# A spectral filter mixed with a product-key memory layer: four of the early row tiles, not two, summed by accumulating TensorE transposes

## The chip, the cores and the metric

One core of a Trainium2 chip runs the whole program. Its engines are TensorE (PE), VectorE (DVE), ScalarE (ACT), GpSimd (POOL) and SyncE (SP); each works through its own queue in order, and they meet by semaphores. The metric is the device time in microseconds (us); the median of three runs is given for the kernel before.

## The reference, cut to what matters

The input x has 2048 rows of 576 numbers. Two branches are computed from it and mixed by a gate per row.

```python
g = sigmoid((x * gate_w).sum(-1))
a = irfft2(rfft2(x) * (w_r + 1j * w_i))               # branch A, over rows and columns
q = einsum("nd,dhc->nhc", x, w_q)                      # branch B: 32 heads, 2 x 128
s1, s2 = q[..., :128] @ k1.T, q[..., 128:] @ k2.T      # 64 scores each
i1, i2 = argmax(s1), argmax(s2);  e = i1 * 64 + i2     # one of 4096 experts per head
act = gelu(sum(x * u[e]));  w = softmax of one score (which is 1)
b = sum over heads of w * act * v[e]
out = g * a + (1 - g) * b
```

So each row and head needs one row of u (for a dot product with x) and one row of v (added, scaled, into the result).

## The kernel before

**Tiles.** The 2048 rows are 16 tiles of 128 rows, one per partition. The 32 heads are 8 chunks `c` of 4. Tiles 0 to 9 are *early* (`E_T`): their branch B runs while scores are still being computed. Tiles 10 to 15 are *late*: theirs runs afterwards, beside branch A.

**Scores.** `build_m` folds w_q and the keys into one matrix per chunk, kept as a high and a low part. `scores(c, tp)` computes chunk c for the two tiles of pair tp: ten *score parts* (`part`), eight of three and two of two 512-column matmuls, 640 parts in all. A reduce on DVE (L415) takes the maxima, ACT compares every score with its maximum (L422), and some DVE and ACT steps turn that into expert numbers (`ei`, `eil`).

**Early groups.** `group(t, c)` handles the four heads of a chunk for one early tile. POOL issues four gathers (L516, 128 rows of 4608 bytes, u and v side by side, into a buffer `uv`); DVE makes four dot products (L523); ACT takes the gelu (L525); a small step makes the four factors `a`. Then the v rows are summed, in one of three ways:

- *by DVE*: one scaled add per row (L553), or, where a bit of `ROWS[t][c]` is set, the row scaled in place by ACT (L548) and added by DVE (L549);
- *by a diagonal* (`is_d`: `ROWS[t][c]` is 16): ACT makes the factors (L535) and writes a 128 x 128 diagonal matrix per row (L563, buffer `dg`); TensorE multiplies it with the row, two matmuls of 288 columns, and accumulates in PSUM; DVE adds the group's sum to the tile's (L577);
- *by transposes* (`lean`, for the tiles in `T_T`): ACT scales the row in place (L499); TensorE transposes it in five pieces of 128 columns, accumulating over the four rows in PSUM; DVE adds the group's sum to a transposed accumulator `xw` (L506; the tile's first group is copied there by ACT, L504). At the end `mix` turns the accumulator back with five more transposes.

In PSUM there are four double banks, shared by all of this: a group by diagonals or by transposes keeps one from its first row to DVE's add.

**Late tiles.** `quad` gathers four rows for 32 tokens at a time (L604), makes the dot products (L609), a block matrix `dg` on DVE (L613), and sums on TensorE. All its gathers wait for the first part of the last score tile (`HELD`).

**Branch A.** `fold` (sums and differences of x, small matmuls), `unit` (transforms, the spectral weights `w`, transforms back) and `invert` (the last transform of a tile) run on TensorE with DVE and ACT between; `mix` and `send` finish a tile.

**Order.** A planner outside the program has fixed the order of all work: every call of `plan` is a job, numbered in program order, and `ORDER` lists the numbers. `follow` gives out buffers in that order, and each engine issues its own jobs in it, the DMAs of SP and POOL too. All matmuls go through the helper at L260, so they are told apart by their tiles: `mh, xt` scores, `dg` diagonals (128*128) and late sums (128*32), `ident,uv` transposes, `fi` transforms.

Of the kernel before, what the change touches and what calls it, by code (L numbers as in the profile page):

```python
# [15 lines left out]
P = 128  # L16
D = 576
# [137 lines left out]
def tile_kernel(ctx, tc, xn, xT, x5, wqT, wq5, kT, wri, uv, gw, t_kr, t_fi, t_tw, t_io, out):  # L155
# [26 lines left out]
    for tag, n in (('cand', 2), ('z', 8), ('b', 8), ('a', 8), ('im', 1), ('fe', 2), ('dg', 3)):  # L182
        ring(tag, 'sm', n)
    ring('uv', 'gp', NG)
    ring('xn', 'xp', 2 * NE - 2 * NPAIR - len(T_T))
    ring('p2', 'ps', 4)
# [299 lines left out]
    accs = {}  # L486
# [146 lines left out]
    def finish(t, pd, sum_of):  # L633

        y = accs[t] = buf(('xl', 'xn'), [P, D])
        ga = gas[t]
        for r in range(2):
            cols = slice(288 * r, 288 * r + 288)
            sum_of(r)
            dv(0.43, lambda r=r, cols=cols: stt(y.ap[:, cols], pd.ap[:, r, :288], gone[:, t:t + 1], ga.ap[:, cols], op0=ALU.mult, op1=ALU.add), [(y, r)], [(pd, r), (ga, 0), (ga, 1), 'gone'])  # L640
            ld(load(P * 1152, 1152), lambda cols=cols: nc.sync.dma_start(out[t][:, cols], y.ap[:, cols]), [], [(y, r)])
# [328 lines left out]
ROWS = {0: (0, 16, 16, 15, 6, 2, 12, 0), 1: (0, 15, 0, 12, 5, 16, 5, 16), 2: (12, 8, 2, 6, 0, 8, 0, 1), 3: (2, 10, 0, 5, 0, 7, 4, 16), 4: (4, 0, 0, 6, 16, 7, 16, 0), 5: (2, 0, 1, 0, 0, 9, 12, 16), 6: (4, 15, 4, 8, 16, 0, 16, 14), 7: (8, 0, 16, 16, 6, 12, 9, 2), 8: (6, 16, 7, 0, 12, 16, 16, 11), 9: (4, 0, 0, 16, 0, 8, 16, 5)}  # L970
SPLIT = 0
T_T = (0,1)
# [17 lines left out]
def is_d(t, c):  # L990
    return t < NE and ROWS[t][c] > 15


ORDER = [
# [214 lines left out]
```

## Time and profile before

| | |
|---|---|
| runs | 898.75, 900.19, 900.25 us; median 900.19 |
| profiled execution | 900.38 us; its span in the trace 898.6 us |
| busy in the span | PE 856.3, DVE 811.5, ACT 596.3, POOL 570.3 us |
| granted TensorE clock, mean | 0.984 |
| moved | 342.44 MB, of which 302.02 by the 512 gathers |

A row of a group of instructions has the line, engine, operation, output and inputs by name, shapes and count; then busy time in us, the mean ns of one, and the idle time of the engine before them. A row of the timeline has the start, the length, the engine, the line and the same names. Busy times overlap a little from one instruction to the next, so what an instruction costs its engine is read from the starts.

### The profile page before, as it was taken

Reading aid. Unit: us, or ns where it says so; the run is one execution under the profiler, and the core shown is the slowest. Engines: PE = TensorE matmul, PEld = TensorE weight load, DVE = VectorE, ACT = ScalarE, POOL = GpSimd, SP = SyncE. Lnnn points to the kernel's source line nnn. Section 1 sums busy time; section 2 is a strip of 40 time slices with the busy share of each in tenths; the row PEclk is TensorE's granted clock in tenths of the full one; section 3 lists DMA queues with packets and bytes.
Section 4 is the critical chain, followed back from the end, with each engine's and each line's share of the span. In section 5 each row is a group of like instructions: output and inputs, shape, how many; then the busy total and the mean of one; then the engine's idle time right before and its main releaser. Section 6 shows DMA issues by size and latency. Waiting matters only on the chain. (4 is left out here: it accounts for less than half of the span.)

```text
span 898.6 us, 16947 instructions
## 1 busy us (share of the span) xinstructions
PE 856.3 (95%) x5502; PEld 661.0 (74%) x5502; DVE 811.5 (90%) x2022; ACT 596.3 (66%) x2067; POOL 570.3 (63%) x516
## 2 busy tenths in 40 slices
PE   6999999999999999999999999769889999899987
PEld 5888888888888778888888888657556676566554
DVE  3779999999999899999999999899999889877877
ACT  4999997877878688788879789773232434232322
POOL 0356556666677676676657776666767677777771
PEclk9999999999999999999999999859999999999999
DMA  9999999999999999999999999999999999999998
GB/s 299 349 332 367 379 345 367 349 372 361 380 357 368 377 386 384 376 388 357 394 359 368 415 350 397 418 370 365 402 415 420 419 402 419 420 420 419 418 419 340
DMA packets 89611, 342.44 MB, mean 381 GB/s; under 512 B 9969, under 2 KB 10865, under 8 KB 89522
## 3 DMA queue, kind: packets, MB, share of 16 engines
q0 software_dynamic: 73728, 302.02, 86.5%
q1 hardware_dynamic: 15794, 39.33, 11.9%
q8 instruction: 44, 0.72, 0.3%
q14 instruction: 45, 0.37, 0.1%
HBM read 336.59 MB, written 4.72 MB: 380 GB/s over the span
## 5 line engine op out<-in xcount | busy, mean ns | idle before, releaser
L516 POOL DMA_INDIRECT uv<-uv,ei x317 | 356.6, 1125 | 226.5 <-issue 46.6
L260 PE MATMUL bank<-mh,xt 128*128 128x512 f32 x768 | 269.8, 402 | 0.0
L422 ACT ACTIVATE area<-bank,area 128x64 bf16<-128x64 f32 x1008 | 220.3, 360 | 15.1 <-DVE area L415 10.9
L604 POOL DMA_INDIRECT uv<-uv,eiq x144 | 156.6, 1087 | 70.1 <-issue 23.3
L523 DVE SCALAR_TENSOR_TENSOR uv<-uv,pair 128x576 f32<-128x576 f32 x256 | 187.3, 750 | 12.5 <-DMA uv<-uv,ei 11.9
L260 PE MATMUL bank<-ml,xt 128*128 128x512 f32 x448 | 175.0, 391 | 0.0
L260 PEld LDWEIGHTS bank<-mh,xt 128*128 128x128 f32 x768 | 144.2, 188 | 30.3
L260 PE MATMUL bank<-mhx,xt 128*128 128x512 f32 x384 | 136.6, 399 | 0.1
L260 PE MATMUL bank<-uv,dg 128*32 128x288 f32 (+1 forms) x784 | 115.0, 412 | 4.3 <-DVE dg L613 4.2
L609 DVE SCALAR_TENSOR_TENSOR uv<-uv,xr 128x576 f32<-128x576 f32 x144 | 105.7, 751 | 12.4 <-DMA uv<-uv,eiq 12.1
L553 DVE SCALAR_TENSOR_TENSOR xn<-uv,a,xn 128x576 f32<-128x576 f32 x133 | 107.7, 811 | 0.2
L260 PE MATMUL bank<-fi,bt 128*128 128x289 f32 x384 | 101.7, 416 | 1.0 <-DVE area L908 1.0
L260 PEld LDWEIGHTS bank<-fi,bt 128*128 128x128 f32 x384 | 82.5, 243 | 20.6 <-issue 6.5
L260 PEld LDWEIGHTS bank<-ml,xt 128*128 128x128 f32 x448 | 84.3, 188 | 15.7
L260 PEld LDWEIGHTS bank<-uv,dg 128*32 128x32 f32 (+1 forms) x784 | 60.6, 131 | 35.7 <-DVE dg L613 10.1
L260 PEld LDWEIGHTS bank<-mhx,xt 128*128 128x128 f32 x384 | 72.1, 188 | 15.6 <-DVE area L371 0.5
L415 DVE TENSOR_REDUCE area<-bank 128x16 f32<-128x1024 f32 x63 | 76.6, 1217 | 4.3 <-PE bank L260 4.0
L260 PE MATMUL bank<-mlx,xt 128*128 128x512 f32 x192 | 75.0, 390 | 0.0
L430 ACT ACTIVATE area<-area 128x256 bf16<-128x256 bf16 x189 | 73.0, 437 | 1.1
L610 ACT ACTIVATE b<-z 128x4 f32<-128x4 f32 x48 | 9.9, 205 | 84.4 <-DVE uv L609 57.9
L260 PEld LDWEIGHTS bank<-kT,uv 128*64 128x64 f32 x1280 | 41.6, 141 | 18.2 <-issue 13.4
L260 PE MATMUL bank<-kT,uv 128*64 128x64 f32 x1280 | 46.5, 228 | 6.7 <-DMA uv<-wqT 6.7
(199 smaller groups left out, 1348.1 us busy)
## 6 DMA issues: line engine op xcount, KB each, us to landing
uv<-wqT SPq DMA_DIRECT2D x32, 512.0 KB, 6.5
uv<-uv,ei POOLq DMA_INDIRECT x317, 6.9
w<-wri SPq DMA_DIRECT2D x16, 289.0 KB, 6.7
pair<-xn SPq DMA_DIRECT2D x8, 288.0 KB, 6.2
uv<-uv,eiq POOLq DMA_INDIRECT x144, 8.6
out<-xn SPq DMA_DIRECT2D x8, 288.0 KB, 5.8
uv<-wq SPq DMA_DIRECT2D x8, 256.0 KB, 6.5
uv<-xT SPq DMA_DIRECT2D x8, 256.0 KB, 7.1
```

What stands on the lines that cost most here:

```text
L260: after('PE', nc.tensor.matmul(*args, **kw))
L415: dv(dve(1024, True), lambda: nc.vector.tensor_reduce(mv.ap[:, 2 * tp:2 * tp + 2, :], ps.ap.rearrange('p a (g e) -> p a g e', e=E), AX.X, ...
L422: on('ACT', actv(sg.ap[:, j, g, :], ps.ap[:, j, g * E:g * E + E], AF.Sign, bias=mv.ap[:, 2 * tp + j, g:g + 1], scale=-1.0))
L430: ac(act(256), lambda b=b: actv(s2()[:, :, b * Q:b * Q + Q], s2()[:, :, b * Q:b * Q + Q], AF.Copy, bias=b / 4), [sg], [])
L516: on('POOL', nc.gpsimd.indirect_dma_start(out=g.ap.rearrange('p a d -> p (a d)'), out_offset=None, in_=uv, in_offset=bass.IndirectOffsetOn ...
L523: dv(0.68, lambda k=k, g=rows[k]: stt(g.ap[:, 0, :], g.ap[:, 0, :], 1.0, x.ap, op0=ALU.mult, op1=ALU.mult, accum_out=z.ap[:, k:k + 1]), [( ...
L553: dv(0.73, lambda v=v, s=s: stt(y.ap, v(), s(), y.ap, op0=ALU.mult, op1=ALU.add), [y], [(rows[k], 1), a])
L604: on('POOL', nc.gpsimd.indirect_dma_start(out=g.ap.rearrange('p a d -> p (a d)'), out_offset=None, in_=uv, in_offset=bass.IndirectOffsetOn ...
L609: dv(0.68, lambda j=j: stt(rows[j].ap[:, 0, :], rows[j].ap[:, 0, :], 1.0, xr[t][j].ap, op0=ALU.mult, op1=ALU.mult, accum_out=z.ap[:, j:j + ...
L610: ac(0.1, lambda: actv(b.ap, z.ap, AF.Gelu_apprx_tanh), [b], [(z, j) for j in range(HPC)], table='gelu')
```

## The change

Tiles 2 and 3 are now summed by transposes too (`T_T`), so the ring of `xn` accumulators has two places fewer and that of `xw` two more. No entry of `ROWS` for the other tiles is 16 any more, so no v row goes through a diagonal. The ring `dg` has two buffers, not three; the last tile's result may also lie in an `xw` buffer; and the order of all jobs is new (4370 jobs, not 4337).

```diff
--- before.py
+++ after.py
@@ -179,7 +179,7 @@
     def ring(tag, pool, n):
         home[tag] = pool
         sizes[tag] = n
-    for tag, n in (('cand', 2), ('z', 8), ('b', 8), ('a', 8), ('im', 1), ('fe', 2), ('dg', 3)):
+    for tag, n in (('cand', 2), ('z', 8), ('b', 8), ('a', 8), ('im', 1), ('fe', 2), ('dg', 2)):
         ring(tag, 'sm', n)
     ring('uv', 'gp', NG)
     ring('xn', 'xp', 2 * NE - 2 * NPAIR - len(T_T))
@@ -632,7 +632,7 @@
 
     def finish(t, pd, sum_of):
 
-        y = accs[t] = buf(('xl', 'xn'), [P, D])
+        y = accs[t] = buf(('xl', 'xn', 'xw'), [P, D])
         ga = gas[t]
         for r in range(2):
             cols = slice(288 * r, 288 * r + 288)
@@ -967,9 +967,9 @@
 EARLY = 4
 LOW_PE = 1
 A_ACT = True
-ROWS = {0: (0, 16, 16, 15, 6, 2, 12, 0), 1: (0, 15, 0, 12, 5, 16, 5, 16), 2: (12, 8, 2, 6, 0, 8, 0, 1), 3: (2, 10, 0, 5, 0, 7, 4, 16), 4: (4, 0, 0, 6, 16, 7, 16, 0), 5: (2, 0, 1, 0, 0, 9, 12, 16), 6: (4, 15, 4, 8, 16, 0, 16, 14), 7: (8, 0, 16, 16, 6, 12, 9, 2), 8: (6, 16, 7, 0, 12, 16, 16, 11), 9: (4, 0, 0, 16, 0, 8, 16, 5)}
+ROWS = {0: (0, 6, 6, 15, 6, 2, 12, 0), 1: (0, 15, 0, 12, 5, 6, 5, 6), 2: (12, 6, 0, 6, 8, 8, 6, 1), 3: (0, 10, 14, 13, 0, 5, 3, 6), 4: (0, 0, 2, 0, 5, 7, 6, 12), 5: (2, 1, 4, 8, 4, 1, 5, 13), 6: (0, 6, 8, 12, 9, 10, 2, 14), 7: (14, 12, 2, 8, 0, 14, 8, 3), 8: (8, 6, 0, 2, 10, 15, 3, 14), 9: (0, 0, 4, 6, 15, 0, 6, 15)}
 SPLIT = 0
-T_T = (0,1)
+T_T = (0,1,2,3)
 NT2 = 4
 NG = 12
 NPAIR = 4
@@ -992,179 +992,181 @@
 
 
 ORDER = [
-    21, 22, 0, 1, 23, 2, 3, 77, 4, 78, 9, 16, 6, 10, 89, 90, 80, 7, 5, 79, 133, 20, 91, 11, 13, 81, 83, 84, 128, 92, 97, 82, 86, 87, 8, 98, 85, 17,
...
-    4328, 4329, 3597, 3778, 4307, 4330, 3617, 3598, 4001, 3779, 4319, 4331, 3599, 3668, 4332, 4333, 4334, 4335, 4336,
+    21, 22, 23, 0, 2, 1, 3, 4, 5, 77, 78, 9, 79, 16, 20, 89, 80, 13, 90, 81, 6, 97, 82, 83, 7, 91, 84, 10, 128, 86, 33, 133, 8, 92, 11, 17, 24, 85,
...
+    4365, 4366, 4368, 4369,
```

Counted in the two lists, this much stands ahead of the 280th, the 320th and the last of the 512 gathers (before / new):

| ahead of gather | 280 | 320 | 512 |
|---|---|---|---|
| score parts, of 640 | 613 / 622 | 640 / 640 | 640 / 640 |
| rows by a diagonal, PE | 39 / 0 | 52 / 0 | 52 / 0 |
| diagonals made, ACT | 40 / 0 | 52 / 0 | 52 / 0 |
| rows by transposes, PE | 56 / 112 | 64 / 128 | 64 / 128 |
| sums of transposed groups, DVE (L506) | 12 / 24 | 14 / 28 | 14 / 28 |
| rows scaled and added, DVE (L553) | 119 / 99 | 132 / 110 | 135 / 111 |
| adds of scaled rows or diagonal groups, DVE (L549, L577) | 59 / 55 | 69 / 67 | 74 / 75 |
| rows scaled, ACT (L499, L548, L551) | 115 / 173 | 129 / 202 | 133 / 209 |
| folds, PE | 0 / 0 | 14 / 13 | 16 / 16 |
| inverts begun, PE | 0 / 0 | 0 / 0 | 16 / 15 |

Of the rows by a diagonal, 44 stand ahead of the last score part and 8 behind it; of those by transposes 60 and 4 before, 112 and 16 now. Ahead of the last score part stand 298 gathers before and 287 now. The first late gather is the 317th before and the 315th now.

344 rows, old and new, of the table ORDER are left out of this document.

## The prediction

> **What bounds the kernel now.** I read the page first, then the busy time of each engine in stretches, then single rows for the price of each step. The stretches are cut where the 280th, the 320th and the last of the 512 gathers are issued. In the stretches each engine has its busy time and (x) its instructions; then come the granted clock, the DMA share and GB/s.
>
> ```profile
> PE 856.3 (95%) x5502; PEld 661.0 (74%) x5502; DVE 811.5 (90%) x2022; ACT 596.3 (66%) x2067; POOL 570.3 (63%) x516
> ```
> ```profile
> 30.00:521.10 491.10, 490.88 (x3245) 403.65 (x3244) 466.54 (x1111) 413.14 (x1512) 314.18 (x279) 1.00 0.98 371
> ...
> 591.10:660.00 68.90, 60.49 (x330) 43.94 (x331) 66.53 (x180) 28.84 (x95) 49.06 (x45) 0.86 0.99 381
> 660.00:882.30 222.30, 212.02 (x1295) 139.32 (x1294) 186.61 (x504) 73.31 (x185) 161.04 (x148) 1.00 1.02 418
> ```
> ```profile
> core 0: us, PE busy (x) PEld busy (x) DVE busy (x) ACT busy (x) POOL busy (x), PEclk, DMA share, GB/s
> 0.00:521.10 521.10, 514.11 (x3474) 422.94 (x3475) 480.80 (x1136) 430.43 (x1554) 314.38 (x283) 1.00 0.98 366
> 521.10:591.10 70.00, 58.83 (x322) 49.39 (x320) 65.39 (x175) 58.82 (x224) 44.37 (x40) 0.94 1.00 390
> 591.10:882.30 291.20, 272.52 (x1623) 183.26 (x1624) 253.15 (x683) 102.16 (x278) 210.10 (x192) 0.97 1.02 409
> 882.30:898.60 16.30, 10.83 (x87) 5.39 (x85) 12.22 (x34) 4.92 (x15) 1.42 (x1) 0.95 0.79 309
> ```
>
> POOL's 279 instructions from 30 to 521.1 are gathers (four smaller ones stand before 30), so the next is the 280th; then it issues 40, 192 and 1. Four stages with different limits follow. Until 521.1 **TensorE sets the pace**: from 30 us it is busy 490.88 of 491.10 us, DVE 95%, ACT 84%. From 521.1 to 591.1 it is **DVE** (65.39 of 70, while PE idles 11 us), and it stays so until 660 (66.53 of 68.90). From 660 on it is **the gathers**: 418 GB/s without a break, while DVE has 36 us to spare. The page's shares of the whole span (PE 95%, DVE 90%) hide these four. The last 16.3 us are the tail. So a microsecond of PE is worth one only before the 280th gather.
>
> **The change part by part.** *Price of a row.* The start of the next instruction on the same engine gives what one costs there.
>
> ```profile
> 249.54 2.10 PE L260 MATMUL bank<-uv,dg 128*128 128x288 f32 x8
> 251.27 0.61 PE L260 MATMUL bank<-mh,xt 128*128 128x512 f32 x1
> ...
> 277.74 2.35 PE L260 MATMUL bank<-ident,uv 128*128 128x128 f32 x20
> 279.84 0.48 PE L260 MATMUL bank<-mhx,xt 128*128 128x512 f32 x1
> ...
> 299.69 0.39 PE L260 MATMUL bank<-ml,xt 128*128 128x512 f32 x1
> 299.92 0.39 PE L260 MATMUL bank<-mh,xt 128*128 128x512 f32 x1
> ```
> ```profile
> 215.59 0.82 DVE L506 TENSOR_TENSOR xw<-bank,xw 128x640 f32<-128x640 f32 x1
> 216.33 0.15 DVE L538 SCALAR_TENSOR_TENSOR a<-b,sw 128x4 f32<-128x4 f32 x1
> 216.40 1.22 DVE L415 TENSOR_REDUCE area<-bank 128x16 f32<-128x1024 f32 x1
> ...
> 300.84 0.75 DVE L549 TENSOR_TENSOR xn<-uv,xn 128x576 f32<-128x576 f32 x1
> 301.51 0.75 DVE L523 SCALAR_TENSOR_TENSOR uv<-uv,pair 128x576 f32<-128x576 f32 x1
> 302.19 0.81 DVE L553 SCALAR_TENSOR_TENSOR xn<-uv,a,xn 128x576 f32<-128x576 f32 x1
> 302.92 1.21 DVE L415 TENSOR_REDUCE area<-bank 128x16 f32<-128x1024 f32 x1
> ```
> ```profile
> 209.00 1.43 ACT L499 ACTIVATE uv<-uv,a 128x576 f32<-128x576 f32 x2
> 210.33 3.37 ACT L422 ACTIVATE area<-bank,area 128x64 bf16<-128x64 f32 x16
> ...
> 249.33 0.40 ACT L563 ACTIVATE dg<-ident,a 128x128 f32<-128x128 f32 x1 [1.64 <-PE bank L260]
> ```
> ```profile
> L535 ACT ACTIVATE a<-b,sw 128x1 f32<-128x1 f32 x52 | 11.0, 283 | 0.3
> ```
>
> PE: a score matmul costs 299.92 - 299.69 = 0.23. Eight diagonal records are two rows: 251.27 - 249.54, plus the 0.22 by which the next matmul (0.61) is longer than its like (0.39), is 1.95, or **0.97 a row**. Twenty transposes are four rows: 279.84 - 277.74 plus 0.09 is 2.19, **0.55 a row**. DVE: a scaled-and-added row (L553) 0.73, an added row already scaled (L549) 0.67, a group's sum out of PSUM (L506) 0.74, the factors (L538) 0.07. ACT: a scaled row 1.33 / 2 = 0.67; a diagonal is busy 0.40, its factor 11.0 / 52 = 0.21.
>
> *Whole kernel.* PE loses 52 diagonal rows (-50.4) and gains 64 transposed ones (+35.2) and two more turns back of five transposes (+1.1): **-14.1**. DVE: 24 rows fewer by L553 (-17.5), 14 more sums by L506 (+10.3), an added row more (+0.7), 13 more factors (+0.9) and about 0 for mixing tiles 2 and 3: **-5.5**. ACT: -52 x 0.61 = -32, +76 scaled rows x 0.67 = +51, two more first copies out of PSUM: about **+20**. Gathers and bytes stay.
>
> *Stage 1, to the 280th gather.* By the table of counts, the new list has 39 diagonal rows fewer ahead of it (-37.8), 56 transposed rows more (+30.8), and nine score parts more: eight of three matmuls and one of two, 26 x 0.23 = +6.0. Sum on PE **-1.0**. The saved time is filled with scores that stood further behind. DVE has 9.6 less there (20 x 0.73 + 4 x 0.67 - 12 x 0.74, the rest factors and folds), which buys nothing, as PE paces; ACT has 58 scaled rows more and 40 diagonals fewer, 58 x 0.67 - 40 x 0.61 = +14, that is 445 of 521, hidden beside PE if spread evenly. I take **-1.0**; the bounds are -1.0 (not less, as PE is full there now), and +6 if each of the 56 added transposed rows holds PE for 0.1 us (the ACT scaling now feeds each, and 28 groups instead of 24 keep a PSUM bank until DVE empties it).
>
> *Stage 2, to the 320th.* PE has 14.6 less there, which is off the path: it idles 11 us already. DVE has 0.9 more (-2 x 0.73 + 2 x 0.67 + 2 x 0.74, less 0.5 for small steps that change sides). Bounds: +0.9 if DVE paces as now; -4.7 if the transfers run at 418 GB/s instead of 390 (70 x 390 / 418 = 65.3), since the scores end earlier. Rows say DVE, so I take **-1.5**.
>
> *Stage 3, to the last gather.* DVE has 2.6 more (-2 x 0.73 + 3 x 0.67, the two tiles' mixing and small steps), PE 2.4 less; both lie mostly beside saturated gathers. Bounds: +2.6, and -6.3 at an even 418 GB/s (291.2 x 409 / 418 = 284.9). I take **-0.5**.
>
> *Tail.* Behind the last gather stands one invert more, with its closing matmuls, so PE has some 4 more beside its 5.5 idle:
>
> ```profile
> 882.91 3.19 PE L260 MATMUL bank<-fi,bt 128*128 128x289 f32 x12
> ```
>
> Bounds 0 and +4; taken **0**, since its cover is the idle time.
>
> *At nothing:* diagonal buffers 3 to 2. Only the late quads and one small spread step use them:
>
> ```profile
> L613 DVE TENSOR_TENSOR dg<-rp,a 128x128 f32<-128x128 f32 x48 | 13.9, 289 | 1.3
> ```
>
> DVE idles 1.3 us before them now; a wait for PE would sit before the dot products queued on DVE, whose 36 spare us after 660 cover 0.7 us for each of 48. One more home for the last result adds no instruction. The loads of the late inputs wait for the last scores and go out some 20 us sooner on SP, with the same bytes.
>
> *Moved waits.* POOL's gathers wait in order for freed rows; PE frees them longest (in total, times, longest):
>
> ```profile
> POOL uv L516 <- PE bank L260: 36.2, 45, 3.1
> ...
> POOL uv L516 <- ACT ei L453: 11.2, 7, 4.5
> ```
>
> It waits only 11.2 us for indices of later scores (L453), so earlier scores open few gathers. A transposed row is freed by PE as a diagonal row was; the rows of tiles 4 to 9 that leave the diagonals are now freed by DVE, in its order.
>
> **Sum:** -1.0 - 1.5 - 0.5 = -3.0 on a span of 898.6; with the 1.8 us around it the profiled execution took 900.4, and the median of the runs is 900.2. Forecast **897.5**.
>
> **The rivals.**
>
> *The saving counts in full.* If PE paced the whole kernel, 14.1 us would go: 886. The 490.88 of 491.10 speaks for it; against it, only 1.0 of the saving lies where PE paces.
>
> *The transfers hide everything.* The DMA share is 0.98 to 1.02 in every stage before the tail; if that is a true limit, stages 2 and 3 keep their length: 899.4, no change. Against it: 390 and 381 GB/s beside 418.
>
> *Slower, by the clock.* Its place is between the last score and 660 us.
>
> ```profile
> 270.00:300.00 30.00, 30.00 (x180) 24.89 (x179) 26.84 (x64) 24.72 (x92) 18.13 (x16) 1.00 0.98 377
> ...
> 570.00:600.00 30.00, 18.34 (x86) 14.58 (x84) 27.69 (x73) 21.38 (x72) 17.53 (x16) 0.72 1.00 385
> ```
>
> Where PE idles, the granted clock falls to 0.72. Stage 2 would have 14.6 us more of idle PE, so 0.72 or less could last to 660. From 591 to 660 PE has 60.49 x 0.86 = 52 us of full-clock work; at 0.72 that is 72 us instead of 68.9, at 0.6 87. It decides from a clock of 0.755 down, and at 0.65 costs 80 - 69 = 11, for which 897.5 + 11 gives 909. For it: the idle time; against it: DVE paces there, so less of PE's work need be done at once. Transposes do not lower the clock where PE is full: 40 of them lie in 270 to 300, at 1.00.
>
> [...]
>
> **How the numbers follow.** Forecast 0.45, full saving 0.12, transfers 0.18, clock 0.25 (with the ACT hold-ups of stage 1, +6, in it). This measurement tells about 0.2%, 1.8 us, from no change. Of the forecast's 0.45, whose bounds reach from -12 to +6.5, 0.34 is faster, 0.09 the same, 0.02 slower; full saving is all faster; transfers give 0.04, 0.11, 0.03; the clock 0.03 the same and 0.22 slower. That is 0.50 faster, 0.23 same, 0.27 slower. The range reaches from the full saving, 886, to the clock at 0.65, 909. The forecast's own range is 888 to 902.
>
> **What would show it.** Right: the 280th gather is still issued near 520 with PE full up to there; the last score's reduce (L415) starts 10 us or more ahead of the 554.6 of before; PE idles more than 11 us in stage 2; the last gather comes 2 to 4 us sooner at 418 GB/s. Wrong: the 280th gather before 515 (then scores or DVE paced) or after 525 (hold-ups by ACT), or a clock under 0.755 between 591 and 660.
>
> ```profile
> L415 DVE TENSOR_REDUCE area<-bank x63: 1207/1216/1226, 30.3 to 554.6; 128x16 f32<-128x1024 f32 x63
> ```

## The result, and the profile after

The changed kernel takes **916.19 us** (median of four runs, 914.32 to 916.51); the kernel before 900.22 (median of four). The ratio is 1.0175, 95% interval 1.0155 to 1.0194: 16 us slower, where 897.5 and at most 909 had been forecast. The profiled execution has a span of 914.2 us.

First the page of the changed kernel (busy time of each engine), then its stretches, cut where the 280th, the 320th and the last gather are issued, and four shorter ones around and behind the end of the scores. Columns as before.

```profile
PE 853.7 (93%) x5624; PEld 663.2 (73%) x5624; DVE 806.8 (88%) x2028; ACT 624.3 (68%) x2041; POOL 570.9 (62%) x516
```
```profile
0.00:526.40 526.40, 516.64 (x3629) 428.00 (x3630) 472.82 (x1130) 457.08 (x1554) 313.90 (x283) 1.00 0.97 362
526.40:602.50 76.10, 54.31 (x286) 46.38 (x284) 69.30 (x185) 58.26 (x193) 44.68 (x40) 0.79 0.97 371
602.50:893.80 291.30, 269.37 (x1619) 181.12 (x1619) 251.57 (x681) 103.98 (x281) 211.07 (x192) 0.97 1.01 405
893.80:914.20 20.40, 13.36 (x92) 7.73 (x92) 13.08 (x35) 4.96 (x15) 1.27 (x1) 0.86 0.70 277
...
540.00:570.00 30.00, 19.22 (x105) 16.80 (x104) 25.54 (x69) 22.69 (x76) 14.98 (x15) 0.72 1.01 398
570.00:600.00 30.00, 19.10 (x115) 17.30 (x113) 27.66 (x80) 25.32 (x81) 18.85 (x17) 0.78 0.95 362
600.00:630.00 30.00, 22.84 (x103) 16.09 (x106) 29.00 (x77) 19.62 (x63) 21.16 (x18) 0.64 0.94 323
630.00:660.00 30.00, 25.46 (x156) 19.14 (x152) 28.56 (x79) 10.76 (x32) 21.38 (x20) 1.00 1.02 405
```

TensorE and DVE are less busy than before (856.3 and 811.5), ACT 28 us more, and the span is 15.6 us longer. TensorE's busy time fell by 2.6 us only, where 14.1 had been forecast. By stage (before / after / difference): to the 280th gather 521.1 / 526.4 / **+5.3**; to the 320th 70.0 / 76.1 / **+6.1**; to the last 291.2 / 291.3 / **+0.1**; tail 16.3 / 20.4 / **+4.1**.

Behind the 280th gather DVE is 3.9 us busier than before (69.30 against 65.39) and idle 2.2 us longer. These are the groups of DVE that differ most there, first before, then after (where the group of L577 is gone), and then one wait of POOL and one of DVE after (what waits for what, then us in total, times, longest):

```profile
L549 DVE TENSOR_TENSOR xn<-uv,xn 128x576 f32<-128x576 f32 x4 | 3.0, 749 | 0.0
L577 DVE TENSOR_TENSOR xn<-bank,xn 128x576 f32<-128x576 f32 x5 | 3.7, 746 | 0.0
...
L506 DVE TENSOR_TENSOR xw<-bank,xw 128x640 f32<-128x640 f32 x2 | 1.6, 822 | 0.5 <-PE bank L260 0.5
```
```profile
L549 DVE TENSOR_TENSOR xn<-uv,xn 128x576 f32<-128x576 f32 x11 | 8.3, 751 | 0.1
...
L506 DVE TENSOR_TENSOR xw<-bank,xw 128x640 f32<-128x640 f32 x4 | 3.3, 818 | 0.0
```
```profile
POOL uv L516 <- ACT bt L755: 6.4, 1, 6.4
...
DVE uv L523 <- DMA uv<-uv,ei: 5.8, 4, 2.4
```

Five sums of whole diagonal groups are gone; seven single added rows and two sums of transposed groups have come. The timeline of the changed kernel shows how that stretch stalls (start, length, engine and line, idle time ahead of it in brackets):

```profile
542.72 0.39 PE L260 MATMUL bank<-ml,xt 128*128 128x512 f32 x1
...
562.61 3.79 PE L260 MATMUL bank<-kr,f 128*128 128x128 f32 x20 [2.31 <-DVE f L743]
...
567.82 4.50 PE L260 MATMUL bank<-ident,uv 128*128 128x128 f32 x20 [1.42 <-ACT uv L499]
```
```profile
560.90 0.76 DVE L523 SCALAR_TENSOR_TENSOR uv<-uv,pair 128x576 f32<-128x576 f32 x1 [2.37 <-DMA uv<-uv,ei]
...
562.85 1.22 DVE L415 TENSOR_REDUCE area<-bank 128x16 f32<-128x1024 f32 x1
```
```profile
563.18 0.94 POOL L516 DMA_INDIRECT uv<-uv,ei  x1 [0.30 <-DMA uv<-uv,ei]
570.48 0.94 POOL L516 DMA_INDIRECT uv<-uv,ei  x1 [6.36 <-ACT bt L755]
```

TensorE ends the scores at 543, 11.5 us sooner than before (554.2). But the reduce of the last score comes at 562.85, 8.2 us later than before (554.63): DVE works in order, and of the 19.8 us between the two it was busy for 15.5 with steps that stand ahead of this reduce and idle for 4.3 in three waits for gathers, the last of them the 2.37 us shown. The folds behind such a wait are late, so TensorE stands 2.31 us; the transposed rows stand behind the folds in TensorE's order and wait for ACT too; and POOL starts no gather for 6.36 us. (The rows follow each other so; that the transposes hold the buffer that this gather wants is read from the order of the rows, not shown by a run.)

### The profile page after: what moved, and what is told of

The parts are those of the page before. It is cut to its first block, busy times and chain, and to the rows that moved or that the text cites. A ratio compares the mean times of both kernels' runs of the same rounds, so it can differ in the third digit from the quotient of the medians.

```text
span 914.2 us, 17202 instructions
## 1 busy us (share of the span) xinstructions
PE 853.7 (93%) x5624; PEld 663.2 (73%) x5624; DVE 806.8 (88%) x2028; ACT 624.3 (68%) x2041; POOL 570.9 (62%) x516
## 5 line engine op out<-in xcount | busy, mean ns | idle before, releaser
L260 PE MATMUL bank<-mh,xt 128*128 128x512 f32 x768 | 266.7, 399 | 0.0
L523 DVE SCALAR_TENSOR_TENSOR uv<-uv,pair 128x576 f32<-128x576 f32 x256 | 188.1, 750 | 20.7 <-DMA uv<-uv,ei 20.4
L609 DVE SCALAR_TENSOR_TENSOR uv<-uv,xr 128x576 f32<-128x576 f32 x143 | 103.6, 751 | 14.0 <-DMA uv<-uv,eiq 8.1
L260 PE MATMUL bank<-fi,bt 128*128 128x289 f32 x384 | 104.2, 424 | 4.6 <-ACT t L918 2.6
L499 ACT ACTIVATE uv<-uv,a 128x576 f32<-128x576 f32 x128 | 93.4, 785 | 6.6 <-DVE a L527 6.4
L260 PE MATMUL bank<-ident,uv 128*128 128x128 f32 x640 | 88.1, 283 | 9.9 <-ACT uv L499 6.4
L260 PEld LDWEIGHTS bank<-ident,uv 128*128 128x128 f32 x640 | 77.4, 146 | 22.3 <-ACT uv L499 9.5
L553 DVE SCALAR_TENSOR_TENSOR xn<-uv,a,xn 128x576 f32<-128x576 f32 x111 | 89.6, 809 | 0.2
L610 ACT ACTIVATE b<-z 128x4 f32<-128x4 f32 x48 | 9.7, 205 | 88.8 <-DVE uv L609 64.2
L260 PE MATMUL bank<-uv,dg 128*32 128x288 f32 x572 | 59.1, 419 | 5.2 <-ACT bt L755 2.8
```

The source lines that it names most:

```text
L260: after('PE', nc.tensor.matmul(*args, **kw))
L499: ac(act_by(576), lambda k=k, v=v: actv(v(), v(), AF.Copy, scale=a.ap[:, k:k + 1]), [(rows[k], 1)], [a])
L523: dv(0.68, lambda k=k, g=rows[k]: stt(g.ap[:, 0, :], g.ap[:, 0, :], 1.0, x.ap, op0=ALU.mult, op1=ALU.mult, accum_out=z.ap[:, k:k + 1]), [( ...
L553: dv(0.73, lambda v=v, s=s: stt(y.ap, v(), s(), y.ap, op0=ALU.mult, op1=ALU.add), [y], [(rows[k], 1), a])
L609: dv(0.68, lambda j=j: stt(rows[j].ap[:, 0, :], rows[j].ap[:, 0, :], 1.0, xr[t][j].ap, op0=ALU.mult, op1=ALU.mult, accum_out=z.ap[:, j:j + ...
L610: ac(0.1, lambda: actv(b.ap, z.ap, AF.Gelu_apprx_tanh), [b], [(z, j) for j in range(HPC)], table='gelu')
```

## The experiments

Three of the comparisons ran on other chips than the rest. There the gathers came slower (from the 320th to the last 311.6 us in e9, 311.7 in e14 and 314.8 in e18, against 289.2 to 296.2 in the table below), and the kernel before itself took 938, 927 and 926 us; those runs are compared with it by ratio alone. The last column of the table is the 95% interval of the ratio. The stages are those of one profiled run each: that of e12 and e11 was the slowest of its runs (2 us over the median), that of e17 the fastest (1.5 under). How far a stage of one profile can be trusted is seen from e5 and e11, which are the changed kernel up to the 280th gather: 525.0 and 525.4 against 526.4.

| run | to 280th | to 320th | to last | tail | median us | ratio |
|---|---|---|---|---|---|---|
| before | 521.1 | 70.0 | 291.2 | 16.3 | 900.2 | 1 |
| changed | 526.4 | 76.1 | 291.3 | 20.4 | 916.2 | 1.016 to 1.019 |
| e3, no scaling for transposes | 523.4 | 76.3 | 290.6 | 19.9 | 912.0 | 1.012 to 1.016 |
| e4, before with late rows | 526.3 | 77.2 | 289.2 | 16.2 | 911.3 | 1.012 to 1.016 |
| e16, e4 without the adds | 520.0 | 69.5 | 292.1 | 16.2 | 899.5 | 0.997 to 1.001 |
| e10, changed without late adds | 523.1 | 71.9 | 291.6 | 20.6 | 909.2 | 1.007 to 1.015 |
| e11, folds issued twice | 525.4 | 80.5 | 293.2 | 19.5 | 918.5 | 1.014 to 1.022 |
| e5, tail reordered | 525.0 | 75.4 | 296.2 | 17.7 | 915.6 | 1.015 to 1.019 |
| e6, middle reordered | 527.8 | 72.9 | 292.2 | 20.9 | 915.6 | 1.015 to 1.019 |
| e12, both ends of the list as before | 524.4 | 77.3 | 292.9 | 17.3 | 911.9 | 1.009 to 1.015 |
| e17, e3, e10 and e12 at once | 521.0 | 72.0 | 290.2 | 18.9 | 905.4 | 1.005 to 1.009 |

**Order or way of summing, swapped whole.** The new settings in the old list, and the old ones in the new list:

```diff
-T_T = (0,1)          # ROWS and ring sizes as before
+T_T = (0,1,2,3)      # ROWS and ring sizes as changed; ORDER: the old one, each new step at the place of the one it replaces
```

> The changed way of summing (four tiles by transposes, no diagonals, the new ROWS, two dg buffers) in the order of before: each new step stands where the step that it replaces stood. Theory A, the order: the 16 us come from where the new list puts the same work, not from the way of summing. Then this kernel loses nothing: 897 to 902 us, the 280th gather issued near 520, the 320th near 590, tail near 16. Theory B, the way of summing: TensorE now waits for ScalarE's scaling row by row and holds PSUM banks longer. Then it is 910 to 918 us whatever the order, with the 280th gather near 526 and PE waits for ACT L499 of 6 us and more. Half and half would be near 908.

> The old way of summing (two tiles by transposes, 13 groups by diagonals, the old ROWS, three dg buffers) in the new order, each step where its counterpart stands in the new list. Theory A, the order: about 912 to 920 us, with the waits of the changed kernel behind the last score (DVE L523 for gathers, POOL for ACT) and its tail of 20 us. Theory B, the way of summing: 898 to 903 us, like before.

Measured: 993.1 and 1001.2 us, ratios 1.104 and 1.113. Neither theory foresaw it, and the question stayed open: a fixed list fits one set of steps, and some 5% of the steps (192 of 4337 go, 225 come) put where others stood cost 10%. The whole loss lies ahead of the 280th gather, issued at 602.1 and 603.4. These are waits of the first of the two, and then two of the same rows in the kernel before:

```profile
ACT b L610 <- DVE uv L609: 59.1, 27, 6.9
POOL uv L516 <- PE bank L260: 56.1, 44, 6.1
...
DVE area L415 <- PE bank L260: 32.6, 22, 4.7
```
```profile
PE bank L260 <- ACT uv L499: 30.3, 5, 11.9
```
```profile
ACT b L610 <- DVE uv L609: 57.9, 26, 6.7
...
DVE area L415 <- PE bank L260: 4.0, 8, 1.3
```

ACT's wait for the dot products is as long as before. New is a chain: TensorE stands 30.3 us for scaled rows (before, this wait is not among its longest, which go down to 1.3), DVE's reduces stand 32.6 for TensorE, and POOL stands 56.1 for TensorE to free rows instead of 36.2.

So most of the later runs change few steps and leave the others where they are.

**Feeding the transposes.**

```diff
-            ac(act_by(576), lambda k=k, v=v: actv(v(), v(), AF.Copy, scale=a.ap[:, k:k + 1]), [(rows[k], 1)], [a])
+            plan('ACT', 0.0, lambda: None, [], [])
```

> The changed kernel with ScalarE's scaling of the transposed rows (L499, 128 instructions, 93 us of ScalarE) left out; the transposes then sum unscaled v rows, so four tiles of branch B are not weighted. Order and all else unchanged. Theory F, feeding: in the first stage TensorE is held up because each transposed row now waits for ScalarE. Then the 280th gather comes back from 526 to 521 to 523 us and the whole to 908 to 912. Rival: the hold-ups have another cause, or ScalarE is not late; then 914 to 917 us, the 280th gather at 525 to 527.

Measured 911.99: 4.2 us less. In the profiled runs 3.0 of them lie before the 280th gather, or 1.6 to 2.0 if e5 and e11 are taken for the changed kernel. The edit leaves out the scaling of all 128 transposed rows, of which the change added 64, and with it 93 us of ACT's work, so it does not part the wait for a scaled row from ACT's load, and its price is an upper bound. In the changed kernel the stalls can be seen one by one (the second below is a wait for ACT's comparison of scores, not for a scaled row); those of TensorE for L499 add up to 1.1 us before the 280th gather. In the kernel before, TensorE is idle for 0.2 us in all from 30 us to that gather.

```profile
341.40 0.77 PE L260 MATMUL bank<-ident,uv 128*128 128x128 f32 x5 [0.34 <-ACT uv L499]
...
472.95 1.15 PE L260 MATMUL bank<-kT,uv 128*64 128x64 f32 x32 [0.43 <-ACT area L422]
...
517.03 0.77 PE L260 MATMUL bank<-ident,uv 128*128 128x128 f32 x5 [0.79 <-ACT uv L499]
```

**Late rows on DVE.** The kernel before with five late groups taken off the diagonals, its list otherwise untouched:

```diff
-ROWS = {..., 4: (4, 0, 0, 6, 16, 7, 16, 0), 5: (..., 16), 6: (..., 16, 14), ...}
+ROWS = {..., 4: (4, 0, 0, 6, 16, 7, 6, 0),  5: (..., 13), 6: (..., 2, 14), ...}    # (4,6) (6,6) (9,6) (8,6) (5,7)
```

> The kernel before, with the last five of its groups by diagonals ((4,6), (6,6), (9,6), (8,6), (5,7)) summed as in the changed kernel, by rows that ScalarE scales or VectorE scales and adds; each new step stands where the step that it replaces stood, and nothing else moves. TensorE loses 20 diagonal rows (19.4 us), VectorE gains 20 adds for 5 group sums, about 11 us. Theory V, VectorE paces from the end of the scores on and the late diagonals were what kept work off it: 906 to 914 us, the 320th gather 8 to 12 us later than the 591 of before, with TensorE idling more. Rival theories (the loss comes from transposes fed by ScalarE, or from the new list): 898 to 902 us.

Measured 911.30: this edit alone makes the kernel before 12 us slower. Up to the 240th gather the two run together (458.0 against 457.8 us); the loss comes behind it. The row of stage 2:

```profile
526.30:603.50 77.20, 43.79 (x236) 38.35 (x236) 72.95 (x189) 59.09 (x213) 46.04 (x40) 0.79 0.95 348
```

DVE is busy 72.95 of 77.20 us, TensorE idles 33.4. To tell DVE's adds from all that changes with them (TensorE's emptiness, its clock, ACT), the same kernel without the 20 adds:

```diff
-                    dv(0.73, lambda v=v, s=s: stt(y.ap, v(), s(), y.ap, ...), [y], [(rows[k], 1), a])
+                    (none if (t, c) in LEFT else dv)(0.73, lambda v=v, s=s: stt(...), [y], [(rows[k], 1), a])    # none: issues nothing
```

> The kernel before with its last five groups by diagonals as scaled rows, as in the run that took 911.3 us, but with VectorE's 20 adds of those groups left out (part of branch B is missing from five tiles; ScalarE still scales its share of the rows). TensorE is as empty as there, VectorE 14 us less loaded. Theory V, the adds on VectorE are what cost those 12 us: 894 to 900 us, the 320th gather near 590 or sooner. Rival, it is TensorE's emptiness (its clock), or ScalarE, or the list that no longer fits: 907 to 912 us.

```profile
520.00:589.50 69.50, 45.73 (x245) 39.22 (x243) 64.53 (x180) 59.57 (x213) 45.09 (x41) 0.82 1.01 401
```

Measured 899.52. TensorE has the same work as in e4 and still idles 23.8 us, its clock is nearly as low (0.82 against 0.79), and the whole loss is gone: it was the adds. From 570 to 600 the clock in this run is even lower than in the changed kernel (0.59 against 0.78), and nothing is lost:

```profile
570.00:600.00 30.00, 19.60 (x79) 15.77 (x80) 28.96 (x77) 24.65 (x80) 18.73 (x17) 0.59 1.00 389
```

The same adds left out of the changed kernel:

> The changed kernel with VectorE's 20 adds of the five late groups (4,6), (6,6), (9,6), (8,6), (5,7) left out (about 14 us of VectorE), so that part of branch B is missing from five tiles; ScalarE's scaling, TensorE's work and the list stay. Theory V, VectorE paces around the end of the scores: the 320th gather comes 6 to 10 us sooner (593 to 597 instead of 602.5) and the whole takes 905 to 909 us. Rival C, the clock: TensorE's low clock (0.64 to 0.78 from 543 to 630) sets the pace; TensorE has the same work, so 914 to 917 us.

> The run without VectorE's 20 adds of the five late groups again, since the kernel before took 938 us beside it the first time (part of branch B is missing from five tiles). Theory V, VectorE paces around the end of the scores: the 320th gather 6 to 10 us sooner than 602.5, the whole 905 to 909 us, a ratio of 1.006 to 1.010. Theory C, the clock sets that stage: 914 to 917 us.

Measured 951.61 beside 938.11 (1.008 to 1.017), then 909.24, 7 us under the changed kernel: 3.3 before the 280th gather (1.9 to 2.3 against e5 and e11) and 4.2 in stage 2. The 20 adds are 14 us of DVE's work, and the change, which took five sums off DVE for them, added 11; so 7 is an upper bound for what they cost there.

**The clock.** Each fold's five matmuls issued twice:

```diff
-            for i in range(ND):
+            for i in (*range(ND), *range(ND)):
                 mm(pf[:, i * P:(i + 1) * P], f.ap[:, i * P:(i + 1) * P], kr.ap, start=True, stop=True)
```

> The changed kernel with every fold's five matmuls issued twice (the second time into the same place, so the result is the same): 16 x 1.1 = 18 us more TensorE work, nearly all between 540 and 605 us, where TensorE idles 22 us and its clock is 0.69 to 0.78. Theory C, the clock: busier TensorE keeps a higher clock, the steps that wait for it come sooner, and the whole falls by 3 us or more, 910 to 913 us, with the 320th gather before 600. Theory V: no gain, 915 to 922 us, as the work is extra and VectorE paces.

> The run with every fold's matmuls issued twice again, for the same reason. In the first one the granted clock from 540 to 630 us was 0.88 to 0.95 instead of 0.64 to 0.78, and the stage was no shorter. Theory V: again no shorter, 915 to 922 us. Theory C: 910 to 913 us.

```profile
540.00:570.00 30.00, 22.61 (x156) 20.43 (x154) 25.12 (x67) 22.87 (x76) 17.32 (x16) 0.83 1.02 404
570.00:600.00 30.00, 21.36 (x164) 19.80 (x162) 23.98 (x67) 21.63 (x70) 16.30 (x16) 0.94 0.88 313
600.00:630.00 30.00, 23.47 (x135) 20.44 (x136) 25.55 (x66) 19.62 (x60) 16.58 (x15) 0.77 0.84 291
```

Measured 959.31 beside 938.11 (1.013 to 1.027), then 918.53. The granted clock rises from 0.72, 0.78, 0.64 to 0.83, 0.94, 0.77, and the stage is 4.4 us longer, not shorter. Together with e16, which has the low clock and no loss, this takes the clock out. (e11 adds TensorE work too, so alone it would not.)

**The list.** The tail alone, the middle alone, then both ends as in the list before:

```diff
-ORDER = [...]    # as changed
+ORDER = [...]    # e5: places from 4058 on rearranged; e6: 2700 to 3493; e12: the first 200 and all behind 3300 in the order of before
```

> The changed kernel with only the list's last 310 places rearranged (156 jobs change places: result DMAs and the last dot products and sums in another order). Theory L, the list: the tail is 20.4 us instead of 16.3 because in-order queues stand behind a late gather; a better order of the same work gives 2 to 3 us back: 913 to 914.5 us with a tail of 18 us. Rival: the tail is longer because of its work (one invert more behind the last gather) or its clock: 915.5 to 917 us.

> The changed kernel with only places 2700 to 3500 of the list rearranged (gathers 265 to 365; some score parts of the last chunk, dot products and folds in another order), the same work. Theory L, the list: behind the last scores VectorE and POOL stand in line for steps that are not ready, and another order gives 3 to 4 us back: 911.5 to 913.5 us, the 320th gather near 599 instead of 602.5. Theory V (the amount of work on VectorE sets that stage): 915 to 917 us.

> The changed kernel (same way of summing) with the first 200 places of its list and all places behind 3300 (gather 335) put in the order of the list before; between them its own list. Theory L, the list at both ends: the 5 us by which it is late at the 20th gather (72.8 against 67.7) are carried to the 280th, and 4 us come in the tail; then the 20th is near 68, the 280th near 522 to 524, and the last stretch from the 360th gather to the end is 245 us instead of 248: 908 to 911 us in all. Rival: TensorE's own work catches up with the late start, and the tail follows from what stands open at the 320th gather: 915 to 917 us.

> The run with both ends of the list put in the order of before again, for the same reason. Theory L, the list at both ends: 908 to 911 us, the 20th gather near 68, the 280th at 522 to 524, from the 360th to the end 245 us instead of 248. Rival, the ends follow from the work: 915 to 917 us. From the first run, whose 20th gather came at 71.2 and whose ratio was 1.014, about 913.

Measured: 915.61 and 915.64, no difference. The tail fell to 17.7 us, but the last gather came 2.7 later; stage 2 fell to 72.9, but its start came 1.4 later. What was won in one stage was given back in the others. Both ends: 950.42 beside 938.11 (1.005 to 1.022), then 911.94, 4.3 us less; the profiled run wins 2.0 to the 280th gather and 3.1 in the tail and gives 2.8 back between. The 20th gather still comes at 72.2, so the late start isn't the list's first 200 places.

**All three at once.**

> The changed kernel with all three causes taken away at once: both ends of the list as before (alone 4.3 us less), ScalarE's scaling of the transposed rows left out (alone 4.2 less), VectorE's 20 adds of the five late groups left out (alone 7.0 less); four tiles are unweighted and five lack rows. If the three add up and are the whole of the 16 us: 899 to 903 us. If they overlap, that is pay for the same wait: 904 to 909.

Measured 905.40. The three don't add up (15.5 alone, 10.8 together): they overlap. In the profiled run, which is 1.5 us under the median, hardly anything of the loss is left up to the last gather (883.2 against 882.4 us); most of what remains is tail, 18.9 against 16.3. This kernel leaves out more work than the change added (see e3 and e10) and is still 5 us slower than the kernel before, so the three do not account for the whole of the 16 us.

**Better versions.**

```diff
-ORDER = [...]
+ORDER = [...]    # e13: changed kernel, e14: the same with (6,7), (8,7) by diagonals, e15: before with (7,7) by a diagonal, (8,5) not; all reworked by small moves
```

> The changed kernel with the same way of summing and a list reworked all along by small moves (from the one with both ends of before), each job at most a few places from where it stood for most. Theory L, most of the 16 us is the list: 905 to 909 us. Theory V plus feeding, the work itself on VectorE and ScalarE: 910 to 914 us, no better than the 911.9 with only both ends changed.

> The changed kernel with two groups of the last chunk, (6,7) and (8,7), put back to diagonals (8 rows; VectorE 8 adds fewer and 2 sums more, about 4 us off it; TensorE 8 us more where it idles), and a list reworked in the same manner. Theory V: 3 to 5 us under the reworked list without diagonals. Rival: the diagonals cost ScalarE and TensorE as much as they save, within 1 us of it.

> The kernel before with one more late group by diagonals, (7,7), one group of the first stage, (8,5), taken off them, and a list reworked by small moves. Theory V: TensorE has 3.9 us less before the 280th gather and VectorE 2 us less behind the scores, 895 to 898 us, under both kernels. Rival: the list of before fits its work so closely that any rework costs more than that, 901 to 908 us.

> The kernel before with one diagonal group of the first stage, (8,5), summed as rows instead (TensorE 3.9 us less where it paces, VectorE 2.2 more) and one more late group, (7,7), summed by diagonals (VectorE 2.2 us less where it paces, TensorE 3.9 more where it idles); each step stands where its counterpart stood, and nothing else moves. By theory V and the pace of TensorE in the first stage: 895 to 899 us, under both kernels. Rival: single groups are too small to be seen, or the list does not fit: 900 to 903 us.

Measured 988.45, 995.46 and 984.91 beside 927.35: ratios 1.065, 1.075 and 1.060. The last, e18, is e15 with the list left alone: 929.95 beside 926.14, 1.003 (1.000 to 1.007). So the rework of the list cost 5 to 6% by itself, as e13 against e9 (1.014, same summing) shows too, and says nothing on the diagonals. The swap of two groups in e18 brought no gain. No version beat the kernel before.

## Why the prediction was wrong

**Stage 1, forecast -1.0, came +5.3.** At the full clock (1.00 up to the 280th gather) the prices held. A transposed row that doesn't wait, and the matmul behind it, in the changed kernel:

```profile
514.52 0.71 PE L260 MATMUL bank<-ident,uv 128*128 128x128 f32 x5
514.98 0.48 PE L260 MATMUL bank<-mh,xt 128*128 128x512 f32 x1
515.30 0.39 PE L260 MATMUL bank<-ml,xt 128*128 128x512 f32 x1
```

514.98 - 514.52 = 0.46, and the next matmul takes 0.32 instead of 0.23: 0.55, as forecast. The failed step is the sum on TensorE, which had its work by places of the list and no wait at all. By the stretches shown, TensorE was busy 516.64 us up to the 280th gather instead of 514.11 (+2.5) and idle 9.8 instead of 7.0 (+2.8). The busy time was mis-sized because the engines do not stand at the same place of the list at the same moment. By 521.1 the kernel before had run 146 diagonal records, four to a row, which is 36.5 rows and not the 39 of the count, so 2.4 us of the saving were not in this stage:

```profile
L260 PE MATMUL bank<-uv,dg 128*128 128x288 f32 x146 | 38.5, 406 | 0.1
```

The waits were there as a bound, +6 for ACT's hold-ups, which was right in kind; I took the other end without a row that spoke for it, and e3 puts the feeding at 3.0 at most. A step that I named and didn't price is that rows leaving the diagonals "are now freed by DVE, in its order"; e10 puts late rows at 3.3 at most there (the two overlap). And I had cut the stage too coarsely. From the 240th gather on, DVE was nearly as full as TensorE in the kernel before:

```profile
457.80:521.10 63.30, 63.30 (x378) 51.83 (x378) 61.35 (x149) 52.74 (x200) 43.66 (x40) 1.00 1.00 386
```

"TensorE sets the pace" was read from one row of 491 us in which DVE has 95%; in its last 63 us DVE has 97%, and e4 shows that an add there costs time.

**Stage 2, forecast -1.5, came +6.1.** That DVE sets the pace there was right, and so was "PE idles more than 11 us" (21.8). The failed step is the term of DVE, "+0.9": it was counted by places of the list between two gathers, and measured 3.9, with 2.2 more idle (by the list two rows of L553 go; in the stretches one comes, x11 before and x12 after). The scores did end 11.5 us sooner on TensorE, but the last reduce came 8.2 us later instead of 10 sooner, because 15.5 us of DVE's own steps and 4.3 us of its waits for gathers stood ahead of it in DVE's order. The late diagonals had been worth much: in e4 about 11 us of DVE's adds cost 12 us of time, while the 8.0 us by which DVE was less busy in stage 1 (472.82 against 480.80) bought nothing to be seen. TensorE's price did not hold here: the twenty transposes at 567.82 took 4.50 us at a clock of 0.72, where the prediction's twenty took 2.35. By e16 the time did not hang on that.

**Stage 3, forecast -0.5, came +0.1.** Right: the gathers pace it (DMA share 1.01, 405 GB/s; 289.2 to 296.2 us in every run of the table).

**Tail, forecast 0, came +4.1.** The bound was +4 and the cover was said to be TensorE's idle time. The cover fails because the last invert doesn't wait for TensorE:

```profile
898.56 4.67 PE L260 MATMUL bank<-fi,bt 128*128 128x289 f32 x12 [2.58 <-ACT t L918]
```
```profile
897.52 0.20 ACT L610 ACTIVATE b<-z 128x4 f32<-128x4 f32 x1 [3.52 <-DVE uv L609]
897.63 0.49 ACT L917 ACTIVATE t<-bank,gsc 128x289 f32<-128x289 f32 x1
```
```profile
896.72 0.76 DVE L609 SCALAR_TENSOR_TENSOR uv<-uv,xr 128x576 f32<-128x576 f32 x1 [2.33 <-DMA uv<-uv,eiq]
```

Its twelve matmuls stand behind ACT's emptying of a bank, that behind a gelu (L610), that behind DVE's dot products, those behind the last gathers. They start 4.7 us after the last gather, and the end comes 15.6 us later; before it was 0.5 (882.91 against 882.4) and 15.7. So the last invert ran behind the last gather in both kernels, whatever its place in the list. With the end of the list as before (e12) it starts 0.6 behind and the tail is 17.3. An invert there was dear where the order of the engines put it behind that gather's own work.

**The range.** Stage 1 and the tail came near their own upper bounds (+6 and +4), stage 2 far over its +0.9. The four upper bounds together are 13.5 us, which is 913.7, but the range ended at 909: it took the slow cases one at a time.

**The rivals.** "Saving in full" and "transfers hide everything" fell. The slower rival had the right sign, and its condition came true in part: the clock was under its 0.755 from 600 to 630 (0.64), but 0.80 over the stretch that it named:

```profile
591.00:660.00 69.00, 54.06 (x278) 40.44 (x280) 66.45 (x179) 38.10 (x119) 48.51 (x43) 0.80 0.98 362
```

Its mechanism did not decide: e16 and e11. The clock was 0.72 from 540 to 570, where transposes and small fold matmuls are all that TensorE has behind 543 and it is busy for 19.22 of 30 us. No run here parts the kind of work from plain idling, and the time didn't hang on it.

**What stays open.** The three causes overlap, so their single prices are not shares, and about 5 of the 16 us are left with all three taken away. The start is late by 5.1 us at the 20th gather (72.8 against 67.7), nearly all of stage 1's 5.3; in between the gathers are late by 2.0 (the 40th) to 7.0 us (the 180th), while TensorE is full from 72 to 240 in both kernels. So how much of stage 1 is start and how much is hold-ups is not parted. The old first places did not undo it (72.2), and two profiled runs with the first places of before differ there by 1.3 (67.7, 69.0). And e17 keeps a tail 2.6 us longer than before with the end of the old list, though its last invert starts 0.5 us behind the last gather, as before; what holds it is not known.

## What to carry to other kernels

Price an edit per stage by the engine that paces that stage, and cut the stages fine enough to see where the pace passes from one engine to the next: here 20 adds moved to DVE late cost 12 us, while 8.0 us less on it early gained nothing to be seen. Count the work of a stage from the trace, not from places in a list: each engine was at another place of it (36.5 diagonal rows run where the list counts 39). A cheaper step on an engine that paces is worth less than it saves if a second engine has to hand it each operand in time: here that took up to 3.0 us of the first stage (e3). Where the order of all work is written out, changed steps need their own order (without it e1 and e2 lost 10 and 11%), and small reworks of it can cost more than the edit (5 to 6% here, where the change cost 1.75%).

## What the runs showed that was not expected

How far a fitted order carries: with 5% of the steps exchanged at their places the kernel lost 10% (e1, e2), and with steps moved a few places 5 to 6% more than with the list left alone (e15 against e18), on chips where the gathers came slower. On such a chip the gathers of the late stage ran at 383 GB/s instead of 418, with the DMA engines as good as always busy (0.98), and the kernel before took 3 to 4% longer:

```profile
660.00:880.00 220.00, 195.27 (x1186) 127.67 (x1186) 172.43 (x461) 67.52 (x168) 144.73 (x136) 0.98 0.98 383
```

That row is of e7. And TensorE's granted clock in the changed kernel went from 0.64 (600 to 630) to 1.00 (630 to 660) with its busy time rising only from 22.84 to 25.46 of 30 us.
